# A sliding-window attention and a long convolution in one kernel: two transfers moved between queues, longer stage rings and a new order of steps

## The chip, the cores and the metric

The kernel runs on one core of a Trainium2 chip. The core has five engines that each take their instructions in order: TensorE (PE) for matrix products, whose weight loads the profile lists apart as PEld, VectorE (DVE), ScalarE (ACT), GpSimd (POOL) and SyncE (SP), which only issues transfers. The metric is the device time of one execution in microseconds (us). An engine stops at an instruction until what that instruction waits for is there, and everything behind it on that engine stops too.

## What is computed

Two independent parts, side by side in the output's columns.

```python
# A: 32 heads of 18, window of 8 positions, every second one
qkv = x @ wqkv                       # x: 2048 x 576
logits[s, w] = (q[s] . k[s - 2 * w]) * 18 ** -0.5     # masked where s - 2 * w < 0
a = (softmax(logits) weighted sum of v[s - 2 * w]) @ wo
# B: a shifted product, then a causal convolution over all 2048 positions
k_shift = sum over t < 4 of k[s - t] * shift_k[:, t]
kv = k_shift * v
y = irfft(rfft(kv, 4096) * rfft(ssm_k, 4096))[:2048] + kv * ssm_D
b = q * y
out = concatenate([a, b], axis=-1)   # 2048 x 1152, bf16
```

## The kernel before

The work is cut into some 400 short steps. Each is a function, and the text `ORDER` at the top lists them as the program is to emit them: `ks.3.0:a` calls `k_spec(3, 0)`, and the letters behind the colon choose the PSUM buffers (a or b, two of each) and the engine that copies the result out (s is ACT, v is DVE, and without either the step's own default, mostly ACT). The loop at lines 667 to 672 walks through this text. Nothing is sorted afterwards: on every engine, and on SyncE's queue, the instructions stand in the order of the text.

**Part A.** `xt` transposes x; `qk` and `qt` project q and k; `v` projects v, one step for two of the 18 elements of a head, into V, whose 16 columns in front of each block of positions are a halo, copied by `vh` (line 393) from the block before. `lm` multiplies q by shifted k on DVE (full ones of 128 x 4096 for h = 0 and 1, a half one for h = 2), `lb` sums the products into logits on PE. `sm` is the softmax, in steps 0 to 6 for each half `hv` of the columns: step 3 subtracts the maximum, step 4 is the exponential on ACT, 5 the sum on PE and its reciprocal on ACT, 6 the scaling on DVE. `pm` multiplies v by the weights (DVE, 128 x 4096, ring Pr of three), `ps` sums that on PE, nine of each for each half. `po` is the output projection for one quarter of the output, 72 pairs of products with one row group each, two copies out of PSUM and two stores from the ring sAr; `pz` is a `po` with the last two `ps` of half 1 put into it, four elements before its end.

**Part B.** The transforms are products with tables, in two stages. `cv` makes kv on DVE; `lkn`, `kw` and `kt` turn ssm_k around through DRAM. `sx` and `kp` are stage one of kv and of ssm_k: three steps each for eight groups, copied into a ring of two (vsr), and the third step writes the group to DRAM (Dx, Dk, line 439). `xl` and `kl` read these back in another layout (lines 546 and 547), into a ring of four slots (Wr) that `yl` shares. A read of Dk needs all eight groups of k to be written. `xs` and `ks` (line 536 on) are stage two, eight of each in two halves; `gp` multiplies the two spectra on DVE; `gi` is the first stage of the inverse, and its second half writes to Dy (line 581). `yl` reads Dy, four reads for each half of the channels, and each of these needs the four writes of its half; `ql` loads q into a ring of four; `ys` is the last stage, two steps for each of the eight, with the product with q on DVE (line 654) and, in the second, the store to the output from the ring ysr.

The order around the change: the first halo copy needs three `v` steps; `gi` needs `gp`, which needs `ks` and `xs`; a `po` needs all `ps` of its half. The last stage-one step of k is `kp.5.2`, and behind it in PE's order come `xs.5.0`, `xs.3.0`, `v.0`, `sm.1.5`, `xs.5.1`, `xs.3.1`, `v.8`, `sm.0.5`, `ps.1.0`, and then `ks.3.0`, the first step that reads k's stage one. At the end stand `ys.5.0` and `ys.5.1`.

Of the kernel before, what the change touches and what calls it, by code (L numbers as in the profile page):

```python
# [15 lines left out]


ORDER = """
tj lx.0.0 lx.0.1 lx.2.0 lwq.1.0 lx.1.0 lx.2.1 lwt lx.1.1 lwq.1.1 lwq.0.1 tv lk.0 lx.3.0 t2 sk.0:a t0 lk.2 sk.2:bv
lx.3.1 sk.1:b xt.0.1:bs xt.0.0:as xt.0.2:bs wm.11:a xt.2.2:as t3 xt.1.2:bs xt.1.0:as qk.1.0.0:b lk.1 xt.2.1:as  # L20
xt.1.1:as xt.2.0:bs t1 tw lwq.0.0 cv.0.0 cv.0.1 t4 qk.1.1.0:b wt qk.1.1.1:a t5 lv.0 lwv lkn.8 lkn.2 lkn.12 lkn.9 lk.3
lkn.13 lkn.4 qk.1.1.2:b xt.3.2:bs qk.0.1.0:a cv.0.3 lkn.6 xt.3.1:bs lkn.7 cv.0.4 lkn.5 lv.1 kw.6 cv.0.2 cv.0.5
xt.3.0:as cv.1.4 cv.0.6 cv.1.0 qk.0.0.2:b cv.1.1 kw.4 lkn.10 cv.0.7 kw.3 qk.0.1.2:b cv.1.3 lkn.14 qk.0.0.1:a sx.0.0:a
sx.0.1:b cv.3.3 cv.1.2 qk.1.1.3:b lkn.15 lkn.0 sx.0.2:a cv.1.5 sx.1.0:a lkn.11 qk.0.1.3:b cv.3.4 sx.1.1:b qt.3:a lkn.1
sx.1.2:b cv.2.1 kw.7 lkn.3 ld qk.0.1.1:a qt.0:b cv.1.6 cv.2.3 kw.0 kw.5 cv.2.4 cv.1.7 qk.0.0.3:b cv.2.0 cv.2.2
sx.2.0:a cv.2.5 kw.2 kw.1 qt.2:b cv.3.5 sx.2.1:a cv.2.6 sx.2.2:b kt.0 cv.3.1 qk.1.0.2:a sx.3.0:b sx.3.1:a kt.1
sx.3.2:b cv.3.0 qt.1:a qk.0.0.0:b qk.1.0.1:a qk.1.0.3:b kp.0.0:a lv.2 cv.3.2 lm.0.2 cv.3.6 kp.0.1:b lm.6.2 lv.3
kp.0.2:a lm.6.1 kp.1.0:b lm.6.0 cv.2.7 kp.1.1:b kp.1.2:a lm.0.0 v.4:a lb.6:a kt.3 kt.2 sx.4.0:b sx.4.1:a lm.0.1 lm.7.0
ia.3 sx.4.2:a sx.5.0:b sx.5.1:b v.2:a ia.5 lb.0:a ia.1 sx.5.2:b kp.2.0:b kt.4 cv.3.7 kp.2.1:a vz kp.2.2:a kt.7 lm.7.1
ia.0 lm.1.0 v.7:b lb.7:b lm.4.1 sx.6.0:a ib sx.6.1:a sx.6.2:b v.1:b sx.7.0:a lm.1.1 sx.7.1:b lm.2.2 sx.7.2:b lb.1:a  # L30
ia.2 lm.4.2 kp.7.0:a lm.4.0 kp.7.1:b xl.3 kp.7.2:b lm.2.1 v.5:a lb.4:b kt.6 kp.3.0:b lm.2.0 kp.3.1:a lm.3.0 kp.3.2:b
im.0 v.3:a kt.5 xl.5 lb.2:b kp.4.0:a kp.4.1:b kp.4.2:b lm.3.1 xl.6 im.1 v.6:a lb.3:a ia.7 kp.6.0:a kp.6.1:b lm.5.0
kp.6.2:a kp.5.0:b lm.5.1 lb.5:av kp.5.1:a sm.1.0 sm.1.1 kp.5.2:b sm.1.2 sm.1.3 xs.5.0:a sm.1.4 xs.3.0:bv ia.4 sm.0.0
v.0:a vh.1 sm.0.1 sm.1.5:a sm.0.2 xs.5.1:a sm.0.3 sm.0.4 xs.3.1:b v.8:a sm.1.6 pm.1.0 pm.1.6 kl.3 sm.0.5:a ps.1.0:b
ks.3.0:a pm.1.3 vh.0 ks.3.1:b gp.3.0 kl.5 gp.3.1 sm.0.6 ps.1.6:a kl.2 ks.5.0:b ks.5.1:a ps.1.3:b pm.0.0 lwo.0 xl.2
kl.0 ks.2.0:a vh.2 ks.2.1:b ia.6 xl.0 lwo.3 gi.3.0:a gi.3.1:b ps.0.0:a gp.5.0 xs.2.0:b gi.5.0:a gp.5.1 pm.1.1 gi.5.1:b
gp.2.0 pm.1.4 xs.2.1:b gp.2.1 ks.0.0:a pm.0.3 xs.6.0:b xl.1 gi.2.0:a ks.0.1:b kl.6 ql.1 xs.0.0:a xs.0.1:b kl.1 lwo.1
gp.0.0 gi.2.1:a ps.1.1:b gp.0.1 ps.0.3:a pm.0.8 xs.1.0:b pm.0.7 gi.0.0:a ks.6.0:b xs.6.1:a kl.7 ps.1.4:bv gi.0.1:a
ks.1.0:b pm.0.1 ks.6.1:a gp.6.0 xl.4 ps.0.7:b gp.1.0 ps.0.8:b ql.3 pm.0.4 xs.1.1:a ks.1.1:b gi.6.0:a ps.0.1:b kl.4
gi.1.0:a gp.6.1 gp.1.1 pm.1.5 pm.0.6 ks.7.0:b xl.7 ql.2 lwo.2 xs.4.0:a gi.1.1:b ps.0.4:a ql.0 ks.4.0:b gi.6.1:a pm.0.5  # L40
xs.7.0:b ps.1.5:av xs.7.1:b ks.7.1:a yl.2 xs.4.1:b ps.0.5:a ps.0.6:b gp.7.0 ks.4.1:a yl.3 yl.1 gi.7.0:b gp.4.0
gi.4.0:a pm.0.2 gp.4.1 yl.0 ps.0.2:b gp.7.1 gi.4.1:a gi.7.1:bv ys.2.0:as ys.2.1:b ys.3.0:as ql.4 ys.3.1:a pm.1.2 yl.4
ql.7 po.0.0.0:v pm.1.8 yl.7 pm.1.7 po.0.1.0 ps.1.2:a ys.0.0:bs ys.0.1:as po.0.0.1:v yl.6 pz.1.0.0 ys.4.0:as ql.6
ys.4.1:as ys.1.0:bs ys.1.1:a ql.5 yl.5 po.1.0.1:v po.1.1.0 ys.7.0:b ys.6.0:as ys.7.1:as ys.6.1:b po.1.1.1:v po.0.1.1
ys.5.0:a ys.5.1:bs
"""


# [1 line left out]
def kernel(  # L50
# [47 lines left out]
    def psb():  # L98
        return psum("b", 2, 512)

    def evac(dst, src, scale=None, on="s"):
        if (how["ev"] or on) == "s":
            nc.scalar.activation(dst, src, ACT.Copy, **({} if scale is None else {"scale": scale}))  # L103
# [442 lines left out]
    def w_load(Dd, key, i):  # L546
        nc.sync.dma_start(Wr.get((key, i)), by_rt(Dd, i // 4, i % 4))
# [20 lines left out]
    def g_inv(i, hv):  # L568
        dh, g = i // 4, i % 4
        Y = Yr[i] if hv else Yr.get(i)  # L570
        for u in range(2):
# [8 lines left out]
        if hv:  # L580
            nc.gpsimd.dma_start(by_rt(Dy, dh, g), Y)
# [121 lines left out]
```

## Time and profile before

| What | us |
|---|---|
| median of 3 runs (208.14 to 210.05) | 208.29 |
| the profiled execution | 211.04 |
| its span | 209.1 |
| PE starts at / its last product ends at | 5.86 / 204.1 |
| granted clock of PE over the span (share of full) | 0.999 |

The span is the profiled execution's time from its first to its last instruction. Busy time is the time in which an engine executes; an instruction that waits is not counted. A line of the waits names the engine and line that waited, what it waited for, the total, the number of times and the longest. In the timeline a line is a run of instructions of one form: start, length, engine, line, operation and tiles, then the idle time before it and what ended that. Line 103 is the helper that copies out of PSUM on ACT, line 105 the same on DVE, so these are told apart by tile sizes and times. The DMA issues give the median time from the issue to the landing of the data.

| Idle of PE by stretch | us |
|---|---|
| 0 to 6 | 5.9 |
| 6 to 52 | 0.3 |
| 52 to 70 | 2.2 |
| 70 to 120 | 4.2 |
| 120 to 160 | 4.0 |
| 160 to 180 | 0.6 |
| 180 to 192 | 0.9 |
| 192 to the end | 5.9 |

### The profile page before, as it was taken

What the parts mean: (1) busy time and instruction counts of PE and PEld (TensorE: products, weight loads), DVE (VectorE), ACT (ScalarE), POOL (GpSimd) and SP (SyncE); (2) the same over time, 40 slices, a digit from 0 to 9 for tenths busy, and PEclk for the clock granted to TensorE, in tenths of its full rate; (3) what the DMA queues carried; (4) which work ended last, traced back from release to release, by engine and by line L of the source; (5) the groups of instructions that cost most, each with busy time, mean ns of one, the idle gap of its engine ahead of it and who ended that gap; (6) DMA issues with size and microseconds to landing.
All of it is one profiled execution on the core that took longest, in us unless ns stands there. A gap on an engine that the chain in (4) does not pass through costs nothing.

```text
span 209.1 us, 6223 instructions
## 1 busy us (share of the span) xinstructions
PE 185.2 (89%) x2645; PEld 118.3 (57%) x2645; DVE 177.8 (85%) x157; ACT 160.7 (77%) x244; POOL 12.9 (6%) x39
## 2 busy tenths in 40 slices
...
GB/s 162 317 316 396 239 211 158 311 198 299 275 368 247 260 181 261 241 214 367 261 250 226 264 242 240 310 350 246 256 390 246 179 330 377 248 335 304 223 314 135
DMA packets 66797, 56.20 MB, mean 269 GB/s; under 512 B 16673, under 2 KB 60306, under 8 KB 66770
## 3 DMA queue, kind: packets, MB, share of 16 engines
...
## 4 chain that ended last, share of the span: by engine, by line
PE 46%; ACT 27%; DMA 16%; issue 6%; DVE 2%; SPq 0%; ACTq 0%; DVEq 0%
ACT area L103 24%; PE psB L377 8%; PE psA L377 5%; DMA Dx<-area 5%; PE psA L610 5%; DMA out_dram<-area 4%; DMA Dy<-area 4%; PE psA L384 3%; PE psA L576 3%; PE psB L599 3%; PE psB L432 2%; DMA Dk<-area 2%; PE psA L599 2%; PE psA L432 2%; DMA area<-in_B_shift_k_dram 2%
## 5 line engine op out<-in xcount | busy, mean ns | idle before, releaser
L103 ACT ACTIVATE area<-psA 128x576 bf16<-128x576 f32 (+7 forms) x117 | 83.5, 757 | 33.1 <-PE psB L610 15.0
L103 ACT ACTIVATE area<-psB 128x576 bf16<-128x576 f32 (+5 forms) x113 | 80.2, 757 | 7.9 <-PE psB L377 4.0
L588 DVE TENSOR_TENSOR area<-area,area 128x4096 bf16<-128x4096 bf16 x18 | 40.6, 2284 | 0.9 <-DMA area<-area 0.8
L487 DVE TENSOR_TENSOR area<-area 128x4096 bf16<-128x4096 bf16 x16 | 35.8, 2286 | 1.0 <-PE psA L504 0.7
L377 PEld LDWEIGHTS <-area 128*128 128x128 bf16 x160 | 15.5, 98 | 17.5
L377 PE MATMUL psB<-area,area 128*128 128x512 bf16 x100 | 23.1, 379 | 0.0
L563 DVE TENSOR_TENSOR area<-area 128x2304 bf16<-128x2304 bf16 x16 | 21.1, 1351 | 1.3 <-ACT area L103 1.0
L461 DVE TENSOR_TENSOR area<-area,area 128x2304 bf16<-128x2304 bf16 x16 | 21.0, 1348 | 0.0
L541 PEld LDWEIGHTS <-W 128*64 128x64 bf16 x256 | 14.0, 108 | 12.3 <-issue 11.1
L610 PE MATMUL psA<-area,area 32*128 32x288 bf16 x288 | 18.7, 281 | 1.6 <-ACT area L103 1.1
L610 PE MATMUL psB<-area,area 32*128 32x288 bf16 x288 | 18.7, 281 | 0.0
L384 PEld LDWEIGHTS <-area 128*32 128x32 bf16 x360 | 15.2, 142 | 5.6 <-issue 2.8
L599 PEld LDWEIGHTS <-ident 64*64 64x64 bf16 x576 | 15.3, 106 | 5.1 <-issue 3.5
L610 PEld LDWEIGHTS <-area 32*128 32x128 bf16 x576 | 15.5, 93 | 4.6 <-issue 2.2
L384 PE MATMUL psA<-area,area 128*32 128x512 bf16 x280 | 16.7, 384 | 0.4 <-ACT area L103 0.2
L432 PEld LDWEIGHTS <-T 128*128 128x128 bf16 x96 | 8.6, 97 | 14.6 <-issue 9.3
L541 PE MATMUL psB<-area,W 128*64 128x288 bf16 x152 | 14.7, 290 | 1.8 <-ACT area L103 1.1
L455 DVE TENSOR_TENSOR area<-area,area 128x2304 bf16<-128x2304 bf16 x12 | 15.8, 1350 | 0.1
L576 PEld LDWEIGHTS <-IAt 64*128 64x128 bf16 x256 | 12.4, 94 | 5.8 <-issue 1.5
L432 PE MATMUL psB<-area,T 128*128 128x384 bf16 x52 | 12.6, 326 | 3.5 <-ACT area L103 3.5
L377 PE MATMUL psA<-area,area 128*128 128x512 bf16 x60 | 13.9, 379 | 0.0
L576 PE MATMUL psA<-area,IAt 64*128 64x288 bf16 x176 | 13.0, 283 | 0.4
...
## 6 DMA issues: line engine op xcount, KB each, us to landing
Dx<-area SPq DMA_DIRECT2D x16, 288.0 KB, 4.2
Dk<-area SPq DMA_DIRECT2D x16, 288.0 KB, 4.4
area<-Dx SPq DMA_DIRECT2D x8, 576.0 KB, 5.9
area<-Dk SPq DMA_DIRECT2D x8, 576.0 KB, 6.8
Dy<-area POOLq DMA_DIRECT2D x8, 576.0 KB, 6.2
area<-Dy SPq DMA_DIRECT2D x8, 576.0 KB, 6.2
area<-in_A_wo_dram SPq DMA_DIRECT2D x4, 648.0 KB, 10.2
area<-in_A_x_dram SPq DMA_DIRECT2D x8, 288.0 KB, 5.4
```

Source lines behind the costliest of these rows:

```text
L103: nc.scalar.activation(dst, src, ACT.Copy, **({} if scale is None else {"scale": scale}))
L377: nc.tensor.matmul(ps[:, u, :], w[:, kb, cols[u]:cols[u] + 128], xT[:, j, kb], start=(kb == 0), stop=(kb == 4))
L384: nc.tensor.matmul(ps[32 * a:32 * a + 32, u, :], wv[:, kb, 2 * n + u:D:DH], xT[:, a, kb], start=(kb == 0), stop=(kb == 4), tile_position=( ...
L432: nc.tensor.matmul(ps[:, ri, 0:384], T1[:, ri, :], sf[:, 384 * ch:384 * ch + 384], start=True, stop=not extra)
L461: nc.vector.tensor_tensor(dst, kfull[:, 4 * c + 3 - j:4 * c + 7 - j, :], skb[:, j, :].unsqueeze(1).to_broadcast([128, 4, D]), ALU.mult)
L487: nc.vector.tensor_tensor(prr.get((n, h)), q2[h], k2[h][:, :, o0:o0 + S], ALU.mult)
L541: nc.tensor.matmul(ps[64 * hp:64 * hp + 64, im, 0:HD], W2[:, im, 8 * g + 2 * prl + hp].rearrange("p l f -> p (l f)"), Wt[:, 2 * prl + hp, ...
L563: nc.vector.tensor_tensor(Pv, Xv.unsqueeze(2).to_broadcast([128, 2, 2, 2 * HD]), Kv.unsqueeze(1).to_broadcast([128, 2, 2, 2 * HD]), ALU.mult)
L576: nc.tensor.matmul(ps[:, hp, 0:HD], IAt[r, tab, 4 * g + 2 * hv + u, :], Pp[(i, hv)][r, n, u, :], start=(n == 0), stop=(n == 3), tile_posit ...
L588: nc.vector.tensor_tensor(Pr.get((hv, p)), vv, Lt[:, :, 256 * hv:256 * hv + 256].unsqueeze(2).to_broadcast([128, W, 2, 256]), ALU.mult)
L599: nc.tensor.matmul(ps[64 * b:64 * b + 64, r, 0:256], ident[g, g], P[g, n, :, 128 * b:128 * b + 128], start=(n == 0), stop=(n == W - 1), ti ...
L610: nc.tensor.matmul(pss[e][:, b, 0:HD], Os[hv][g, d // 2, r, 128 * (d % 2):128 * (d % 2) + 128], wo4[g, d, d0:d1], start=(d == 0), stop=(d ...
```

## The change

Two transfers change their queue: the three halo copies of V and the eight writes of the inverse's first stage are issued from SyncE, where before GpSimd issued them. The ring of stages for the second output's last products has four slots where it had two, and that of the projection's copies has nine where it had six; the new slots lie in an area that the kernel did not use any more at that time. The list of steps holds the same steps in another order, some of them with another PSUM buffer or another engine for the copy.

```diff
 ORDER = """
...
-kp.6.2:a kp.5.0:b lm.5.1 lb.5:av kp.5.1:a sm.1.0 sm.1.1 kp.5.2:b sm.1.2 sm.1.3 xs.5.0:a sm.1.4 xs.3.0:bv ia.4 sm.0.0
-v.0:a vh.1 sm.0.1 sm.1.5:a sm.0.2 xs.5.1:a sm.0.3 sm.0.4 xs.3.1:b v.8:a sm.1.6 pm.1.0 pm.1.6 kl.3 sm.0.5:a ps.1.0:b
-ks.3.0:a pm.1.3 vh.0 ks.3.1:b gp.3.0 kl.5 gp.3.1 sm.0.6 ps.1.6:a kl.2 ks.5.0:b ks.5.1:a ps.1.3:b pm.0.0 lwo.0 xl.2
...
-gi.4.0:a pm.0.2 gp.4.1 yl.0 ps.0.2:b gp.7.1 gi.4.1:a gi.7.1:bv ys.2.0:as ys.2.1:b ys.3.0:as ql.4 ys.3.1:a pm.1.2 yl.4
-ql.7 po.0.0.0:v pm.1.8 yl.7 pm.1.7 po.0.1.0 ps.1.2:a ys.0.0:bs ys.0.1:as po.0.0.1:v yl.6 pz.1.0.0 ys.4.0:as ql.6
-ys.4.1:as ys.1.0:bs ys.1.1:a ql.5 yl.5 po.1.0.1:v po.1.1.0 ys.7.0:b ys.6.0:as ys.7.1:as ys.6.1:b po.1.1.1:v po.0.1.1
-ys.5.0:a ys.5.1:bs
+lx.1.0 lx.1.1 tj t0 lx.3.1 t2 lx.3.0 xt.1.2:as tv lx.0.1 sk.0:b xt.1.0:as sk.1:a xt.3.0:bs lx.2.1 lx.2.0 t3 lx.0.0
+wm.11:b lwt xt.1.1:a sk.2:b xt.2.2:bs xt.2.0:as xt.0.1:bs lwq.1.1 xt.0.0:bs tw xt.2.1:a qk.1.1.1:a lk.0 xt.0.2:bs
...
+kp.6.1:bv kp.6.2:a lb.4:a lm.5.1 im.0 kp.7.0:b kp.7.1:a xl.3 kp.7.2:b v.5:a kp.3.0:a lm.2.1 kp.3.1:bv lb.2:b kp.3.2:a
+vh.2 kl.3 im.1 kl.0 xs.0.0:b lm.5.0 lm.3.0 vh.1 v.1:a lb.5:a xs.3.0:b ia.4 lm.3.1 xs.3.1:av lb.3:b xs.0.1:b ks.3.0:b
+ks.0.0:a sm.1.0 sm.0.0 sm.1.1 ib sm.0.1 sm.1.2 sm.1.3 sm.1.4 gp.3.0 ql.6 v.2:b kl.1 ql.3 sm.0.2 gp.0.0 xl.1 sm.1.5:a
+vh.0 sm.0.3 sm.1.6 ks.3.1:b gi.0.0:a gp.3.1 sm.0.4 pm.1.2 xs.1.0:b gi.3.0:a sm.0.5:b pm.1.0 sm.0.6 ks.0.1:a lwo.1
+gp.0.1 kl.5 ql.2 pm.0.8 xs.1.1:b ps.1.2:a ia.6 lwo.2 ks.1.0:b xl.5 gi.0.1:a gp.1.0 ks.5.0:b kl.2 pm.0.1 gi.3.1:a
+ks.5.1:b xl.6 ps.1.0:a pm.0.2 ks.1.1:b gp.1.1 ps.0.8:a xs.5.0:b gi.1.0:a xs.5.1:b pm.0.0 xl.2 ps.0.1:a kl.4 gi.1.1:b
...
+ps.0.3:b ps.0.6:a gp.2.0 gp.2.1 gi.2.0:b ql.1 kl.7 xs.4.0:av ks.4.0:b gp.6.1 pm.0.7 gi.2.1:a ks.4.1:b gi.6.1:a
+xs.4.1:b xs.7.0:av ps.0.7:b gp.4.0 xs.7.1:a ks.7.0:b yl.1 gp.4.1 pm.1.1 yl.0 yl.2 ks.7.1:a gi.4.0:b gp.7.0 gi.4.1:a
+ps.1.1:b gp.7.1 po.0.0.1 yl.3 ys.1.0:b pm.1.3 gi.7.0:a gi.7.1:b ys.2.0:as ys.1.1:bs ql.0 pm.1.5 po.0.1.1 pm.1.4
+po.0.1.0 yl.7 ys.0.0:as ys.3.0:bs ys.2.1:as ps.1.4:b ps.1.3:b pm.1.8 ql.7 yl.4 ps.1.5:b ys.3.1:a ys.0.1:bs pm.1.7 yl.6
+ql.5 yl.5 ql.4 po.0.0.0 pz.1.0.0:s ys.7.0:a po.1.1.1 ys.6.0:b ys.4.0:as ys.7.1:a ys.6.1:bs ys.4.1:bs ys.5.0:a ys.5.1:b
+po.1.0.1 po.1.1.0
 """
...
-    ysr = Ring(mk.take(4, HD), mk.take(4, HD))
+    r9.reset()
+    ysr = Ring(mk.take(4, HD), mk.take(4, HD), r9.take(4, HD), r9.take(4, HD))
     smt = [mk.take(2304) for _ in range(2)]
-    sAr = Ring(*[r.take(2, HD) for r in (r1, r5, r6, r1, r5, r6)])
+    sAr = Ring(*[r.take(2, HD) for r in (r1, r5, r6, r1, r5, r6, r9, r9, r9)])
...
     def v_halo(g):
         d = slice(6 * g, 6 * g + 6)
-        nc.gpsimd.dma_start(V[32:128, d, 0:PADL], V[0:96, d, 512:VT])
+        nc.sync.dma_start(V[32:128, d, 0:PADL], V[0:96, d, 512:VT])
...
         if hv:
-            nc.gpsimd.dma_start(by_rt(Dy, dh, g), Y)
+            nc.sync.dma_start(by_rt(Dy, dh, g), Y)
             Yr.drop(i)
```

Copies that the new order gives to DVE: `xt.1.1`, `xt.2.1`, `kp.0.1`, `sx.7.0`, `kp.6.1`, `kp.3.1`, `xs.3.1`, `xs.4.0` and `xs.7.0`, and those of seven `ys` steps. In the old order these were `sk.2`, `lb.5`, `xs.3.0`, `ps.1.4`, `ps.1.5`, `gi.7.1`, the four `po` with a v, the last `ps` inside `pz`, and those of six `ys` steps.

More of the change, by code (lines that the diff above doesn't have):

```diff
@@ L18 @@
 ORDER = """
[L19 to L32, printed above, removed]
-kp.6.2:a kp.5.0:b lm.5.1 lb.5:av kp.5.1:a sm.1.0 sm.1.1 kp.5.2:b sm.1.2 sm.1.3 xs.5.0:a sm.1.4 xs.3.0:bv ia.4 sm.0.0
@@ L34 @@
-v.0:a vh.1 sm.0.1 sm.1.5:a sm.0.2 xs.5.1:a sm.0.3 sm.0.4 xs.3.1:b v.8:a sm.1.6 pm.1.0 pm.1.6 kl.3 sm.0.5:a ps.1.0:b
-ks.3.0:a pm.1.3 vh.0 ks.3.1:b gp.3.0 kl.5 gp.3.1 sm.0.6 ps.1.6:a kl.2 ks.5.0:b ks.5.1:a ps.1.3:b pm.0.0 lwo.0 xl.2
-kl.0 ks.2.0:a vh.2 ks.2.1:b ia.6 xl.0 lwo.3 gi.3.0:a gi.3.1:b ps.0.0:a gp.5.0 xs.2.0:b gi.5.0:a gp.5.1 pm.1.1 gi.5.1:b
-gp.2.0 pm.1.4 xs.2.1:b gp.2.1 ks.0.0:a pm.0.3 xs.6.0:b xl.1 gi.2.0:a ks.0.1:b kl.6 ql.1 xs.0.0:a xs.0.1:b kl.1 lwo.1
-gp.0.0 gi.2.1:a ps.1.1:b gp.0.1 ps.0.3:a pm.0.8 xs.1.0:b pm.0.7 gi.0.0:a ks.6.0:b xs.6.1:a kl.7 ps.1.4:bv gi.0.1:a
@@ L39 @@
-ks.1.0:b pm.0.1 ks.6.1:a gp.6.0 xl.4 ps.0.7:b gp.1.0 ps.0.8:b ql.3 pm.0.4 xs.1.1:a ks.1.1:b gi.6.0:a ps.0.1:b kl.4
-gi.1.0:a gp.6.1 gp.1.1 pm.1.5 pm.0.6 ks.7.0:b xl.7 ql.2 lwo.2 xs.4.0:a gi.1.1:b ps.0.4:a ql.0 ks.4.0:b gi.6.1:a pm.0.5
-xs.7.0:b ps.1.5:av xs.7.1:b ks.7.1:a yl.2 xs.4.1:b ps.0.5:a ps.0.6:b gp.7.0 ks.4.1:a yl.3 yl.1 gi.7.0:b gp.4.0
-gi.4.0:a pm.0.2 gp.4.1 yl.0 ps.0.2:b gp.7.1 gi.4.1:a gi.7.1:bv ys.2.0:as ys.2.1:b ys.3.0:as ql.4 ys.3.1:a pm.1.2 yl.4
-ql.7 po.0.0.0:v pm.1.8 yl.7 pm.1.7 po.0.1.0 ps.1.2:a ys.0.0:bs ys.0.1:as po.0.0.1:v yl.6 pz.1.0.0 ys.4.0:as ql.6
@@ L44 @@
-ys.4.1:as ys.1.0:bs ys.1.1:a ql.5 yl.5 po.1.0.1:v po.1.1.0 ys.7.0:b ys.6.0:as ys.7.1:as ys.6.1:b po.1.1.1:v po.0.1.1
-ys.5.0:a ys.5.1:bs
+lx.1.0 lx.1.1 tj t0 lx.3.1 t2 lx.3.0 xt.1.2:as tv lx.0.1 sk.0:b xt.1.0:as sk.1:a xt.3.0:bs lx.2.1 lx.2.0 t3 lx.0.0
+wm.11:b lwt xt.1.1:a sk.2:b xt.2.2:bs xt.2.0:as xt.0.1:bs lwq.1.1 xt.0.0:bs tw xt.2.1:a qk.1.1.1:a lk.0 xt.0.2:bs
+lwq.0.0 xt.3.2:bs qk.1.1.2:a cv.0.0 cv.0.3 lwq.0.1 t4 lwq.1.0 qk.0.0.2:b wt qk.0.0.0:a lk.1 cv.0.1 lwv xt.3.1:bs lk.2
+t1 cv.0.4 cv.1.4 cv.0.5 lv.0 ia.2 cv.0.2 qt.2:a lv.1 qk.0.1.0:a cv.0.6 cv.1.3 lkn.6 cv.0.7 cv.1.1 lkn.4 lkn.7 lkn.14
@@ new lines @@
+lk.3 lkn.12 cv.1.0 lkn.15 cv.2.3 cv.1.2 kw.3 qk.0.0.3:b cv.1.5 lkn.0 cv.2.1 qk.1.0.1:a lv.2 lkn.1 lkn.8 kw.7 sx.0.0:b
+cv.1.6 lkn.9 sx.0.1:a qt.3:b cv.1.7 cv.3.4 sx.0.2:a qk.1.0.0:b cv.2.4 kw.0 qt.1:a lkn.10 sx.1.0:a lkn.11 sx.1.1:b
+v.0:b lkn.5 sx.1.2:b cv.2.0 cv.3.3 cv.2.2 cv.2.5 qk.0.1.3:a sx.2.0:a cv.3.1 lkn.2 sx.2.1:b kw.5 ld kw.2 qk.1.0.2:b
+sx.3.0:a lkn.13 kw.4 lkn.3 sx.2.2:b cv.2.6 qk.1.1.0:a qk.0.1.2:a cv.3.5 kw.6 cv.2.7 sx.3.1:b kw.1 ia.1 sx.3.2:a cv.3.0
+qk.0.0.1:b kt.1 cv.3.2 sx.4.0:a vz kt.0 qk.1.0.3:b qt.0:b cv.3.6 lm.6.0 lv.3 sx.4.1:a sx.4.2:a lm.0.2 lm.0.0 t5
@@ new lines @@
+qk.0.1.1:b ia.5 kp.1.0:a kp.1.1:a kp.1.2:b cv.3.7 qk.1.1.3:b kp.0.0:a kt.2 kp.0.1:av kp.0.2:b lm.0.1 v.3:b lm.6.2 ia.3
+sx.5.0:a lb.0:b kt.4 sx.5.1:b lm.6.1 ia.7 sx.5.2:a lm.7.0 sx.6.0:a sx.6.1:b sx.6.2:b lb.6:a lm.7.1 ia.0 v.7:a
+sx.7.0:bv kt.5 lm.1.0 sx.7.1:a sx.7.2:b lb.7:a kp.2.0:b kp.2.1:a kp.2.2:b xl.0 kt.6 lm.4.2 lm.1.1 v.4:a kp.4.0:b
+kp.4.1:a kp.4.2:b v.6:a lm.4.0 lb.1:a kp.5.0:b kp.5.1:b lm.2.2 kt.7 kp.5.2:a lm.4.1 v.8:a lm.2.0 kp.6.0:b kt.3
+kp.6.1:bv kp.6.2:a lb.4:a lm.5.1 im.0 kp.7.0:b kp.7.1:a xl.3 kp.7.2:b v.5:a kp.3.0:a lm.2.1 kp.3.1:bv lb.2:b kp.3.2:a
```

2 lines of the change are left out of this document (added).

## The prediction

> **What bounds the kernel now.** I read the page's busy times first, then the engines' busy time by stretches of the span, the waits (the SyncE queue's own too), the DMA issues, and last the timeline at two places. Engine totals:
>
> ```profile
> PE 185.2 (89%) x2645; PEld 118.3 (57%) x2645; DVE 177.8 (85%) x157; ACT 160.7 (77%) x244; POOL 12.9 (6%) x39
> ```
>
> No engine is idle enough to be free. Where the time is lost shows in the stretches (length, then busy time of PE, PEld, DVE, ACT, POOL):
>
> ```profile
> 6.00:52.00 46.00, 45.66 (x266) 23.96 (x265) 40.59 (x48) 37.85 (x48) 0.92 (x5) 1.00 1.08 271
> ...
> 70.00:120.00 50.00, 45.82 (x660) 29.12 (x660) 45.80 (x32) 45.09 (x64) 2.37 (x3) 1.00 0.99 252
> 120.00:160.00 40.00, 36.02 (x634) 25.34 (x635) 37.97 (x24) 38.70 (x72) 2.74 (x5) 1.00 1.02 283
> 160.00:180.00 20.00, 19.44 (x427) 15.17 (x426) 18.53 (x18) 14.05 (x26) 1.60 (x3) 1.00 0.93 296
> ```
>
> Until 52 us TensorE (PE) is the bound. From 70 to 160 three engines are above 90% and PE loses 8.2 us to the others; from 120 to 160 ScalarE (ACT) is at 97%, VectorE (DVE) at 95%. After 170 PE leads again. So a new order gains only where it removes waits between engines that are all nearly full. The waits the edits aim at:
>
> ```profile
> POOL Dy L581 <- ACT area L103: 50.8, 7, 10.7
> ...
> DVE area L654 <- DMA out_dram<-area: 4.2, 2, 2.1
> ...
> ACT area L103 <- DMA out_dram<-area: 1.0, 1, 1.0
> ```
>
> The first is GpSimd waiting in front of the inverse's writes, for results that ACT has not yet copied; nothing else is queued there. The others are the two stages of the second output, held by their stores. What a write followed by a read through DRAM costs (KB each, us to landing):
>
> ```profile
> Dk<-area SPq DMA_DIRECT2D x16, 288.0 KB, 4.4
> ...
> area<-Dk SPq DMA_DIRECT2D x8, 576.0 KB, 6.8
> Dy<-area POOLq DMA_DIRECT2D x8, 576.0 KB, 6.2
> area<-Dy SPq DMA_DIRECT2D x8, 576.0 KB, 6.2
> ```
>
> And one such passage in the timelines of PE and SyncE, from the last stage-one product of k to the first spectrum of k:
>
> ```profile
> 103.07 0.49 PE L432 MATMUL psB<-area,T 128*128 128x384 bf16 x2
> ...
> 102.72 4.07 SPq L439 DMA_DIRECT2D Dk<-area  x4
> ...
> 108.59 3.70 SPq L547 DMA_DIRECT2D area<-Dk  x3
> ...
> 115.61 0.71 PE L541 MATMUL psA<-area,W 128*64 128x288 bf16 x8
> ```
>
> The product ends at 103.5, its write is out at 106.8, the first read starts at 108.6, and ks.3.0 runs at 115.6: 12.1 us.
>
> **Three stages.** I cut the span at the start of ks.3.1 (116.1), the end of gi.7.1 (171.8) and the last matmul (204.1); the last store ends it at 209.1. So 116.1 + 55.7 + 32.3 + 5.0. For each stage I add each engine's steps in both orders. Durations are from start to start on a full engine: on PE, 2.2 for a v, 1.2 for an lb, 0.70 for an xs or ks, 1.03 for a gi, 1.02 for a ps, 2.23 for a po, 0.52 for a ys, 0.98 for the softmax sum; on ACT, 0.69 for a 768-wide copy, 1.06 for the two of an xs, ks, gi or po, 0.49 for a ps; on DVE, 2.2 for a pm or a full lm, 1.27 for a gp, 0.67 for a 576-wide copy.
>
> **First stage.** PE now starts on quarter 1's transposes. Their two loads are issued first, at 0.8 and 1.3; with the 5.4 us that x loads take they are there at 6.3 to 6.7, where before PE began at 5.86: +0.5. Two transposes' copies and four stage-one copies go to DVE. DVE has no 768-wide row: 0.69 for 512 and 0.75 for 576 put it at 0.9; the least is 0.75, the most 1.5 for two 576s. ACT is relieved of 4 x 0.69 = 2.8, of which I count 1.0 on the path (none to 2.8), since DVE is as full. Ahead of k's last product the new order has the same number of v steps (seven) but two lb fewer: -2.4. So that product ends at 103.5 + 0.5 - 1.0 - 2.4 = 100.6.
>
> Here lies the main cost. Before, PE had xs.5.0, xs.3.0, v.0, sm.1.5, xs.5.1, xs.3.1, v.8, sm.0.5 and ps.1.0 to do in the 12.1 us: 10.2 of work. Now it has xs.0.0, v.1, lb.5, xs.3.0, xs.3.1, lb.3 and xs.0.1: 7.4, and ks.3.0 stands in front of v.2 and sm.1.5. PE idles 4.7 in place of 1.9. vh.2's halo copy, now on SyncE, stands between the write and the read, but SyncE waits 1.8 there for the write anyway, and its issue (0.36 to 1.6 among SyncE's rows, 0.75 on GpSimd) mostly fits. ks.3.0 is at 112.7; with ks.0.0, v.2 and sm.1.5 (4.6 with ks.3.0), ks.3.1 comes at 117.3. [...]
>
> **Second stage.** PE before: 27 xs or ks, 16 gi, 14 ps = 49.7. After: 26, 16, 13, and sm.0.5, po.0.0.1 and ys.1.0: 51.7. ACT: 50.4 before (27 and 15 doubles, 12 ps), 52.5 after (24 and 16 doubles, 13 ps, a softmax exponential, po's copies). DVE up to what gi.7.1 needs: 49.1 before, 51.0 after (xs.4.0 and xs.7.0 add 2.7). Before, the stage took 5.3 more than its fullest engine's sum. ACT is still the fullest; 52.5 + 4.5 = 57.0, a little less than 5.3 because ACT and PE are closer to even. From 54.5 (2 over the sum) to 59.5.
>
> The eight inverse writes now cost SyncE 8 x 0.5 (the Dx rows) = 4.0 of issue. SyncE is idle in waits for far longer, so that is hidden. What counts is that SyncE stands at each until ACT has copied: behind gi.0.1 waits kl.2, behind gi.3.1 xl.6, behind gi.5.1 xl.7, behind gi.6.1 yl.1. Counting PE work between where a load can be issued and its use, kl.2, xl.6 and xl.7 keep over 8 us, more than the 6.8 they take: nothing. xl.2, which waits for a slot and not for a write, keeps 5.5, about a microsecond short: in the range. Landing should be as from GpSimd: same-sized reads on SyncE take 5.9 to 6.8, against 6.2.
>
> **Third stage.** PE: 29.2 before; 28.5 after (15 ys, 7 po, 5 ps). The trace took 3.1 more. More stages remove the idle PE had at 197 to 199, 0.9 us; nine projection stages are worth nothing, since no projection copy waits for a store. But ql.0 now needs the slot that ys.1.1 frees, and its product comes two pm later: 0.45 + 6.9 - 4.4 = 3.0 of DVE idle, and pm.1.8 and pm.1.7 are behind it. DVE then needs 14.0 and a lag of 1.2 from ys.1.1 to the end of pm.1.7; PE has 14.1 before the sum that needs it: 1.1 late. 28.5 + 3.1 - 0.9 + 1.1 = 31.8. The end: a po's two copies (1.3) and a store (3.6) take what ys.5.1 took: 5.0.
>
> **Sum.** 117.3 + 57.0 + 31.8 + 5.0 = 211.1, against a span of 209.1: +2.0. (The profiled execution lasted 211.04 with 1.9 around its span; the median of the runs is 208.29.) 208.3 + 2.0 = 210.3.
>
> **Rivals.** *Faster: the loads land early.* The Dk read's shortest row is 4.9 and ACT may lag 1.3 instead of 2.4; then the passage is 9.1, and PE, which lb.3 holds for some 1.4 until DVE's lm.3.1, is hardly idle: -3.0. With a second stage at its lower bound, -2.5: 204.8. For it: ACT is lighter; against: three engines above 90% seldom drop to 2 us of loss. [...]
>
> *Slower: SyncE's order holds y.* yl.1 needs Dy of gi.2.1: ACT's lag 1.5, issue 0.5, write 6.2, issue 0.4, read 6.2 = 14.8; with the longest rows (7.8, 8.1) 18.3. PE has 11.6 of work from gi.2.1 to ys.1.0, 12.8 with the stage's usual idle. Beyond that everything stops, since gi.7.0, gi.7.1 and pm.1.3 are behind ys.1.0. 2.0 to 5.5, of which I have counted some 0.5 in the second stage: +3.0, 213.3. Before, gi.1.1 had over 14 us to ys.2.0. [...]
>
> *Nothing: the waits removed and added cancel,* as they would with a k read of 5.5: 208.5.
>
> **Chances.** Forecast 0.40 (208.5 to 212), half of it beyond 1%; faster 0.28; slower 0.24; nothing 0.08. A measurement of this kernel tells about 1% from no change, so: faster 0.28, same 0.28, slower 0.44. The range, with the unknown bounds on both sides, is 204.5 to 214.5.
>
> **What would show it.** Right: a gap of 3 us or more on PE ahead of the first ks, a DVE wait of 2 to 3 us for q in the tail, no DVE or ACT wait on a store. Wrong: ks.3.0 running straight after xs.0.1, or ACT under 90% between ks.3.1 and gi.7.1 with PE full.

## The result, and the profile after

| What | before | after |
|---|---|---|
| median of four executions, us | 209.04 | 215.94 |
| lowest to highest | 208.14 to 210.05 | 214.28 to 217.30 |
| profiled execution / its span | 211.04 / 209.1 | 216.25 / 214.5 |
| start of ks.3.1 | 116.1 | 115.3 |
| from there to the end of gi.7.1 | 55.7 | 62.3 |
| from there to the last matmul | 32.3 | 31.0 |
| from there to the end | 5.0 | 6.0 |

The time after is 1.0325 times the time before, 95% interval 1.023 to 1.042. Each ratio below is against executions of the kernel before on the same chip at the same time, and leaves out executions over 1.5% above their kernel's fastest, which the kernel before shows too (9 of 26 in one series); where that took several of a new kernel's, they are listed. The whole loss is in the second stage. The engines' busy time over the span has hardly changed:

```profile
PE 186.5 (87%) x2645; PEld 115.7 (54%) x2645; DVE 176.5 (82%) x152; ACT 162.3 (76%) x248; POOL 6.1 (3%) x28
```

The stretches of after (length, then PE, PEld, DVE, ACT, POOL busy, granted clock, the DMA engines' busy share, GB/s; that share is the packets' time over that of 16 engines and passes 1 in the first row), first those that were shown of before, then slices of 2 us:

```profile
6.00:52.00 46.00, 44.38 (x291) 23.44 (x290) 42.95 (x45) 35.88 (x46) 0.60 (x4) 1.00 1.10 285
70.00:120.00 50.00, 43.98 (x594) 24.73 (x587) 47.04 (x34) 42.49 (x60) 0.00 (x0) 1.00 0.93 251
120.00:160.00 40.00, 34.06 (x634) 24.45 (x635) 39.00 (x24) 35.77 (x67) 0.00 (x0) 0.98 0.99 279
160.00:180.00 20.00, 19.12 (x340) 13.44 (x340) 12.86 (x13) 16.29 (x30) 0.00 (x0) 0.95 0.64 203
...
156.00:158.00 2.00, 0.00 (x0) 0.00 (x0) 2.00 (x4) 0.00 (x0) 0.00 (x0) 1.00 0.94 346
158.00:160.00 2.00, 1.27 (x10) 0.78 (x11) 2.00 (x2) 0.54 (x1) 0.00 (x0) 0.68 0.11 35
160.00:162.00 2.00, 2.00 (x18) 1.05 (x16) 0.28 (x1) 1.31 (x3) 0.00 (x0) 0.50 0.00 0
```

In 160 to 180 PE did 340 matmuls where it did 427 before. At 156 to 158 it did none, and from 158.7 to 162.1 it ran at half clock. PE's timeline there (start, length, operation, count, idle before and what ended it):

```profile
154.91 0.68 PE L542 MATMUL psA<-area,W 128*64 128x288 bf16 x8
158.73 1.17 PE L542 MATMUL psB<-area,W 128*64 128x288 bf16 x8 [3.14 <-issue]
159.84 2.10 PE L577 MATMUL psA<-area,IAt 64*128 64x288 bf16 x16
```

The idle time stands ahead of ks.4.0, and its releaser is "issue": no data, no slot and no copy that the profile knows of. The k that it reads was asked for at 135.4. The gi behind it took 2.10 us, where others take 1.15.

Of the waits that the edits aimed at, DVE's and ACT's for stores are gone from the list. The inverse writes' wait now stands on SyncE, shorter than the 50.8 us on GpSimd:

```profile
SPq L582 <- ACT area L103: 28.1, 8, 11.4
```

The transfers' rows (KB each, us to landing): the writes of k and Dy land earlier than before, the reads of x later.

```profile
Dk<-area SPq DMA_DIRECT2D x16, 288.0 KB, 3.9
area<-Dx SPq DMA_DIRECT2D x8, 576.0 KB, 7.6
area<-Dk SPq DMA_DIRECT2D x8, 576.0 KB, 6.7
Dy<-area SPq DMA_DIRECT2D x8, 576.0 KB, 4.9
area<-Dy SPq DMA_DIRECT2D x8, 576.0 KB, 5.7
area<-in_A_wo_dram SPq DMA_DIRECT2D x4, 648.0 KB, 8.6
```

What "issue" hides can be read from the DMA queues. One of them is named "instruction":

```profile
q1 hardware_dynamic: 68448, 55.81, 94.0%
q8 instruction: 20, 0.33, 0.7%
```

It carries 20 packets of 16,384 B in the span. Between two of their starts PE does 256 matmuls and weight loads on average, and the 20 of them cover nearly all of its 5,290, so they are read here as PE's own instructions, piece by piece. Call each matmul or weight load a row, and count the requests from 0: at quiet times request j starts where PE runs row 202 + 256 j (202 fitted to the trace of before; 33 of the 40 requests of before and after started no more than 2.5 us behind that point). Request 11 of after started at 156.25, 6.1 us behind that point, and PE had stopped at 155.6 with its 1,629th matmul, 240 rows past the point: by this reading it had nothing left to run. Every trace here has the same stop. In none of 17 did PE start the next row sooner than 1.2 us after the end of that request's packet (323 cases), and 25 times it stood for 0.3 to 3.7 us exactly there and went on 1.2 to 1.7 us after that end (four more times it went on over 3.3 us after, with a copy of ACT's as the releaser). SyncE's queue, what it had issued in the 10 us ahead:

```profile
146.35 0.32 SPq L582 DMA_DIRECT2D Dy<-area  x1
146.72 1.68 SPq L273 DMA_DIRECT2D area<-in_A_wo_dram  x1
149.16 0.32 SPq L548 DMA_DIRECT2D area<-Dx  x1
149.58 0.38 SPq L642 DMA_DIRECT2D area<-in_B_q_dram  x1
150.07 1.26 SPq L548 DMA_DIRECT2D area<-Dk  x1
```

A write, the 648 KB of `lwo.0` (one of four loads of the projection's weights, which have their places in the list of steps) and three more loads, about 2.6 MB, lie ahead of the request at 150.

### The profile page after: what moved, and what is told of

The parts are those of the page before. It is cut to its first block, busy times and chain, and to the rows that moved or that the text cites. A ratio compares the mean times of both kernels' runs of the same rounds, so it can differ in the third digit from the quotient of the medians.

```text
span 214.5 us, 6194 instructions
## 1 busy us (share of the span) xinstructions
PE 186.5 (87%) x2645; PEld 115.7 (54%) x2645; DVE 176.5 (82%) x152; ACT 162.3 (76%) x248; POOL 6.1 (3%) x28
## 4 chain that ended last, share of the span: by engine, by line
DMA 30%; PE 22%; ACT 22%; SPq 8%; DVE 8%; issue 7%; ACTq 1%; DVEq 0%
ACT area L103 19%; DMA area<-Kt 5%; PE psA L611 5%; DMA Dx<-area 4%; DMA area<-in_B_v_dram 4%; DMA area<-in_B_k_dram 4%; SPq L263 4%; DMA Dk<-area 3%; PE psA L577 3%; DMA area<-Dk 3%; DMA area<-in_A_x_dram 2%; DVE area L589 2%; PE psB L600 2%; DVE area L462 2%; ACT area L527 2%
## 5 line engine op out<-in xcount | busy, mean ns | idle before, releaser
L103 ACT ACTIVATE area<-psA 128x576 bf16<-128x576 f32 (+6 forms) x110 | 78.5, 743 | 29.3 <-PE psB L611 9.9
L103 ACT ACTIVATE area<-psB 128x576 bf16<-128x576 f32 (+8 forms) x124 | 85.5, 731 | 14.5 <-PE psB L542 3.7
L462 DVE TENSOR_TENSOR area<-area,area 128x2304 bf16<-128x2304 bf16 x16 | 21.2, 1353 | 0.6 <-DMA area<-in_B_k_dram 0.4
L542 PE MATMUL psB<-area,W 128*64 128x288 bf16 x168 | 16.5, 300 | 5.5 <-issue 3.1
L378 PE MATMUL psA<-area,area 128*128 128x512 bf16 x80 | 18.6, 379 | 1.5 <-ACT area L103 1.5
L378 PE MATMUL psB<-area,area 128*128 128x512 bf16 x80 | 18.6, 379 | 0.0
L385 PEld LDWEIGHTS <-area 128*32 128x32 bf16 x360 | 13.5, 141 | 6.7 <-issue 2.4
L456 DVE TENSOR_TENSOR area<-area,area 128x2304 bf16<-128x2304 bf16 x11 | 14.6, 1353 | 0.1
L385 PE MATMUL psA<-area,area 128*32 128x512 bf16 x240 | 14.3, 383 | 0.0
L577 PE MATMUL psA<-area,IAt 64*128 64x288 bf16 x176 | 13.8, 298 | 0.0
L433 PE MATMUL psB<-area,T 128*128 128x384 bf16 x48 | 11.4, 327 | 2.0 <-DVE area L105 0.8
```

The source lines that it names most:

```text
L378: nc.tensor.matmul(ps[:, u, :], w[:, kb, cols[u]:cols[u] + 128], xT[:, j, kb], start=(kb == 0), stop=(kb == 4))
L385: nc.tensor.matmul(ps[32 * a:32 * a + 32, u, :], wv[:, kb, 2 * n + u:D:DH], xT[:, a, kb], start=(kb == 0), stop=(kb == 4), tile_position=( ...
L433: nc.tensor.matmul(ps[:, ri, 0:384], T1[:, ri, :], sf[:, 384 * ch:384 * ch + 384], start=True, stop=not extra)
L462: nc.vector.tensor_tensor(dst, kfull[:, 4 * c + 3 - j:4 * c + 7 - j, :], skb[:, j, :].unsqueeze(1).to_broadcast([128, 4, D]), ALU.mult)
L542: nc.tensor.matmul(ps[64 * hp:64 * hp + 64, im, 0:HD], W2[:, im, 8 * g + 2 * prl + hp].rearrange("p l f -> p (l f)"), Wt[:, 2 * prl + hp, ...
```

## The experiments

### Is it the instructions?

**wo_moved.** The load in front is moved away.

```diff
-... sm.0.6 ks.0.1:a lwo.1
+... sm.0.6 ks.0.1:a lwo.1 lwo.0
-... xs.6.1:b lwo.0 xl.7 ...
+... xs.6.1:b xl.7 ...
```

> One load is moved: lwo.0, the projection's weights of group 0 (648 KB), stands right behind lwo.1 and not ahead of xl.7. Theory (late instructions): PE's instructions come by DMA in pieces of 16 KB, 256 instructions each; the piece that ks.4.0 needs was asked for 6.1 us late, because the load lwo.0 lay in front of it, and PE ran dry. Then the gap of 3.4 us in ks.4.0 and the half clock after it go: no PE idle over 2 us between ks.3.1 and gi.7.1, granted clock 1.0 there, second stage 57 to 58 in place of 62.1, time 209.5 to 211.5. The request at about 118 may be late instead, but it has 6 us to spare. Rival (a wait of ks.4.0 for data, a slot or a copy): gap where it was, 215 to 217.

Measured: 211.48, 211.99, 215.81 and 217.12, against 208.91; the ratio of the two lower ones is 1.0157 (1.007 to 1.024). The profiled execution is the 217.12, so no trace shows one that gained: request 11 is 2.4 us late, PE has no gap at ks.4.0, the clock is full, and still the second stage takes 61.4. In it PE waits 2.0 us for Dk, 0.8 for Dx and ACT 1.1 for a write of Dy. The dry PE at ks.4.0 went with the load, and in this execution other waits took its place.

**rows_shifted.** The profile of after has a weight load for each of its matmuls (2,645 of both), so five matmuls fewer are ten rows.

```diff
-wm.11:b lwt xt.1.1:a
+wm.6:b lwt xt.1.1:a
```

> Five of the eleven warm-up matmuls of the first microseconds are left out (their result is read by nobody), so that every later PE instruction stands 10 rows earlier in the program. Theory (late instructions): the pieces of 256 are cut 10 rows later in the order of steps, so the gap moves: it opens inside ks.4.0 after some 5 of its matmuls instead of before the first, and stays 3 to 4 us long; time 214 to 217. Rival (a wait of ks.4.0's first matmul): the gap stays ahead of that matmul. Both expect the half clock behind the gap.

Measured: 216.41, 1.0365 (1.028 to 1.045). PE's timeline:

```profile
156.83 0.68 PE L542 MATMUL psA<-area,W 128*64 128x288 bf16 x8
157.35 0.68 PE L542 MATMUL psB<-area,W 128*64 128x288 bf16 x5
159.96 0.40 PE L542 MATMUL psB<-area,W 128*64 128x288 bf16 x3 [1.94 <-issue]
160.30 1.73 PE L577 MATMUL psA<-area,IAt 64*128 64x288 bf16 x16
```

The eight matmuls of ks.4.0 are cut in two, five ahead of the gap and three behind it, as the theory asks of a shift by five. A wait for data, a slot or a copy can't do that: it would stand ahead of the first or, for the second of the step's two PSUM buffers, of the fifth. The gap was again followed by half clock (160.7 to 164.1).

**halo_pool.** Only the halo copies go back to GpSimd.

```diff
-        nc.sync.dma_start(V[32:128, d, 0:PADL], V[0:96, d, 512:VT])
+        nc.gpsimd.dma_start(V[32:128, d, 0:PADL], V[0:96, d, 512:VT])
```

> The kernel after with the halo copies back on GpSimd; the inverse writes stay on SyncE. In the run with both on GpSimd the halo copy landed late and DVE stood 3.0 us for it ahead of pm.1.2. Theory (late instructions behind the burst at 146, which the inverse write on SyncE makes; halo late as well): the gap in ks.4.0 as in after, and DVE's wait for the halo beside it: 215 to 218. Rival (the halo copy on SyncE is what costs the time, as in the run with the order kept): 210 to 212.

Measured: 216.95, 1.0369 (1.028 to 1.046), as the theory said. The gap stands at the same matmul (profiled at 218.85):

```profile
158.48 0.68 PE L542 MATMUL psA<-area,W 128*64 128x288 bf16 x8
162.87 1.17 PE L542 MATMUL psB<-area,W 128*64 128x288 bf16 x8 [3.71 <-issue]
```

The request was 6.2 us late. DVE waited 2.3 us for a halo copy. The nine profiles in the new order, by how late request 11 was (the profile puts the idle time of pool_queue and wo_late down to ACT, but both end 1.4 us after the packet):

```
kernel        request 11 late   idle of PE at that row
halo_pool          6.2                3.7
after              6.1                3.1
rows_shifted       5.3                1.9
pool_queue         4.2                1.2
wo_late            3.6                0.7
wo_moved           2.4                none
dy_pool_wo         2.4                none
wo_pieces          2.4                none
after_no_wo        1.9                none
```

### What the queues and the rings do

**pool_queue.** Both transfers go back to GpSimd, in the new order.

```diff
-            nc.sync.dma_start(by_rt(Dy, dh, g), Y)
+            nc.gpsimd.dma_start(by_rt(Dy, dh, g), Y)
```

and the halo copies as in halo_pool.

> The order and rings of after, but the halo copies and the inverse writes go out from GpSimd as before. Theory (late instructions): SyncE no longer stands 4 to 11 us at the writes, so loads are issued when their slot is free, one by one and not in a burst at 146 to 151; lwo.0 goes out several us earlier and clear of the request at 150: gap gone, 209.5 to 212. Rival (the order itself makes ks.4.0 wait): gap of 3 us stays, 215 to 217. Rival (SyncE's order as such costs time beyond the gap): under 209.

Measured: 211.41, 214.88, 215.27 and 215.75, too far apart for a ratio. The theory's gap-free 209.5 to 212 is missed: request 11 was still 4.2 us late. The profiled execution (215.75) lost more elsewhere: DVE waited 3.0 us for a halo copy, its products came late, and PE stood 2.9 us at a gi for them.

**order_kept.** The old list of steps with the new queues and rings (diff: ORDER of before).

> The queues and rings of after with the order of steps of before. Theory (late instructions, set by where the projection's weights and the inverse writes fall in the new order): no gap over 2.5 us on PE between ks.3.1 and gi.7.1; time 207.5 to 210, since the rings take away the stores' waits in the third stage (0.9) and little else changes. Rival (the moved writes hold SyncE and cost the time whatever the order): 212 to 216.

Measured: 212.67, 1.0224 (1.013 to 1.032): the rival's number, and by one clear wait. SyncE's queue and PE, in that kernel:

```profile
SPq L394 <- DVE area L589: 3.9, 1, 3.9
```

```profile
111.43 0.61 SPq L394 DMA_DIRECT2D area<-area  x1
112.15 1.04 SPq L548 DMA_DIRECT2D area<-Dk  x2
```

```profile
118.76 1.17 PE L542 MATMUL psB<-area,W 128*64 128x288 bf16 x8 [3.32 <-DMA area<-Dk]
```

SyncE stood 3.9 us at a halo copy until DVE was done; the two k reads behind it went out late, and PE waited 3.3 us for one of them. 6.8 us of half clock followed.

**rings_only.** Old order, old queues, the larger rings alone.

> The order and queues of before with only the two larger rings (four stages for ys, nine for po). Theory (the rings take away the waits on stores in the third stage and nothing else): 207.5 to 209, no wait of DVE or ACT on a store. Rival (a ring changes where other waits fall, as the whole change did): over 211.

Measured: 210.10, 1.0031 (0.999 to 1.007): no difference that the measurement can tell. The waits on stores are gone. In the profiled execution, the slowest of the ten, ACT waited 2.3 us for a write of Dy near 133; why the 0.9 does not show in the other nine is open.

**kept_halo_pool.** As rings_only, with the inverse writes on SyncE.

> The order of before, the larger rings, the inverse writes on SyncE, but the halo copies on GpSimd as before. It parts the two queue moves in the run with the order kept, where SyncE stood 3.9 us at vh.0 for DVE and the k reads behind it came late: PE waited 3.3 us for Dk at 115.4 and two windows of half clock followed. Theory (the halo copy held SyncE): no such wait, no half clock inside the span, 208 to 210. Rival (the inverse writes hold SyncE): 211 to 214 as with both.

Measured: 210.62, 1.0078 (1.003 to 1.013). So in the old order the halo copies on SyncE cost some 3 us (order_kept against this one, 3.8 and 0.7 above their references), and the eight inverse writes about 1 or nothing: the intervals of this kernel and of rings_only overlap. The half clock did not go, though: it stands once, from 105.7, behind 2.1 us in which PE waited for ACT.

### What else can be late

**dy_pool_wo.** wo_moved, with the inverse writes on GpSimd.

> The order and rings of after with lwo.0 right behind lwo.1, the inverse writes on GpSimd, the halo copies on SyncE. Theory (late instructions from the burst behind the inverse write, and, with both transfers on GpSimd, a late halo copy that held DVE 3.0 us): neither is left, so no PE idle over 2 us between ks.3.1 and gi.7.1, all executions near 209.5 to 211.5. Rival (the new order itself is some 3 us longer in the second stage): 212 to 215 with no single gap.

Measured: 216.67, 1.0329 (1.025 to 1.041), all executions between 216.2 and 218.2. Both are missed, by the time and by the single gap: ACT stood 2.8 us because a stage of gi was still being written to Dy, PE stood behind it, and half clock followed (139.2 to 142.7). The last write ahead of that had gone out at 131.5; a weight load and three other loads had in the 10 us before. That they made it late is likely, not shown.

**wo_pieces.** The four weight loads in three parts each, the twelve spread over the list from ks.0.1 to kl.7.

```diff
-    def load_wo(g):
-        nc.sync.dma_start(wo4[32 * g:32 * g + 32], A_wo.rearrange("(h d) n -> h d n", d=DH), max_dma_last_dim=2304)
+    def load_wo(g, k):
+        d = slice(6 * k, 6 * k + 6)
+        nc.sync.dma_start(wo4[32 * g:32 * g + 32, d], A_wo.rearrange("(h d) n -> h d n", d=DH)[:, d, :], max_dma_last_dim=2304)
```

> The kernel after with each of the four loads of the projection's weights (648 KB) cut into three of 216 KB, which are spread over the order from the place of lwo.1 to that of kl.7. The same bytes, no long load. Theory (a long load holds up the requests for instructions): no request after 115 us is late by over 4 us, no dry PE in ks.4.0; 209.5 to 212, and no execution over 214. Rival (the traffic as such makes them late, or something other than lwo.0): 213 to 217.

Measured: 215.91, 1.0311 (1.023 to 1.039): the rival. No request after 115 us was over 3.5 us late, and PE did not run dry at ks.4.0. In place of that it waited for operands:

```profile
143.53 0.68 PE L543 MATMUL psB<-area,W 128*64 128x288 bf16 x8 [2.84 <-DMA area<-Dx]
...
151.97 0.80 PE L543 MATMUL psB<-area,W 128*64 128x288 bf16 x8 [3.00 <-DMA area<-Dk]
```

So the instructions were the victim in after, not the cause. Something makes one transfer or another late by 3 us whichever way the loads are laid. The stretches of before show a candidate that the prediction had in front of it and passed over (the last two columns: the DMA engines' busy share, GB/s):

```profile
115.00:158.00 43.00, 38.57 (x698) 27.46 (x692) 40.97 (x26) 41.67 (x78) 3.64 (x6) 1.00 1.02 286
158.00:172.00 14.00, 13.58 (x258) 9.68 (x256) 12.87 (x9) 13.53 (x25) 1.10 (x3) 1.00 0.88 249
```

And of after:

```profile
115.00:158.00 43.00, 36.62 (x676) 25.98 (x674) 41.88 (x28) 40.00 (x73) 0.00 (x0) 1.00 1.02 287
158.00:172.00 14.00, 12.72 (x184) 8.38 (x183) 9.43 (x8) 11.18 (x21) 0.00 (x0) 0.88 0.49 164
```

The DMA engines are full until 158 in both (1.02). The old order still keeps them busy after that (0.88), the new one does not (0.49, and 0.57 in wo_moved, where PE does not stand at ks.4.0): it asks for its loads sooner, in a stretch in which the engines are already full.

**before_wo_pair and before_wo_three.** The old order with weight loads pushed together at 138 us.

```diff
-... xs.0.1:b kl.1 lwo.1
+... xs.0.1:b kl.1 lwo.1 lwo.2
```

and for the second `kl.1 lwo.3 lwo.1 lwo.2`, each taken from its old place.

> The kernel before with one load moved the other way: lwo.2 goes out right behind lwo.1 (at about 138 in place of 152), so that 1.3 MB is under way when PE asks for the piece of instructions after 144. Theory (late instructions): that request, 1.1 us late before, is 4 to 8 us late, PE runs dry near 150 for 1 to 3 us with no data, slot or copy as releaser, and a window of half clock may follow; 210 to 215. Rival (loads do not hold up instructions): 207.5 to 210, no such gap; if kl.7 lands late instead, PE waits for Dk there.

> The kernel before with three of the four weight loads in a row (lwo.3, lwo.1, lwo.2, 1.9 MB from about 138 us). With two in a row the request for instructions after 144 was 3.4 us late and had 1.6 us to spare. Theory (late instructions): late by over 5 us now, PE dry at its 1,500th matmul, near 150 us, for 1 to 4 us, with no data, slot or copy as releaser; 210.5 to 215. Rival (loads do not hold up instructions): no gap at that matmul, or one that Dk or Dx releases; 208 to 211.

Measured: 210.92, 1.0018 (0.997 to 1.007), and 212.65, 1.0205 (1.013 to 1.028). Two executions of the pair's ten are left out (212.52 and 212.74). The request after 144 came 3.4 and 3.7 us late. PE ran dry where the theory said, near its 1,500th matmul, with "issue" as the releaser, but for 0.4 us in the first and 0.9 in the second, less than the 1 us that was the least expected. The line of the second:

```profile
148.19 0.41 PE L599 MATMUL psB<-area,ident 64*64 64x256 bf16 x8 [0.90 <-issue]
```

So the mechanism shows in the old order too, and its price there was set too high. A larger wait of the second: a write of Dy came late and held ACT for 2.0 us.

**after_no_wo, before_no_wo, before_more.** Loads taken out of the stretch, and put in.

```diff
-        nc.sync.dma_start(wo4[32 * g:32 * g + 32], A_wo.rearrange("(h d) n -> h d n", d=DH), max_dma_last_dim=2304)
+        if g == 1:
+            nc.gpsimd.memset(wo4.rearrange("p d n -> p (d n)").bitcast(FP32), 0.0)
```

in the first two, and in before_more, to the order of before:

```diff
-... pm.0.7 gi.0.0:a ks.6.0:b ...
+... pm.0.7 gi.0.0:a lwo.0 ks.6.0:b ...
-gi.1.0:a gp.6.1 gp.1.1 ...
+gi.1.0:a lwo.3 gp.6.1 gp.1.1 ...
```

> The kernel after without the four loads of the projection's weights (2.6 MB between 115 and 155 us): GpSimd sets them to zero instead, so the first output is zeros. All instructions of PE, ACT and DVE stay. Theory (the DMA engines are full between 115 and 158, and the new order asks for more there than they bring): requests for instructions are at most 3 us late, no PE idle over 2 us between ks.3.1 and gi.7.1, no half clock, 208 to 211. Rival (the new order as such): a gap of the same size, 214 to 217.

> The control: the kernel before without the four weight loads, zeros from GpSimd in their place. Theory (the DMA engines are full here too, but the order of before is fitted to it): a gain smaller than in the new order, 206.5 to 208.5. If the new order is as good as the old one but for the traffic, the two come out within 2 us of each other; if it is worse in itself, it stays 4 us or more above.

> The kernel before with two of the weight loads made twice (lwo.0 again behind lwo.1, lwo.3 again ahead of xl.7): 1.3 MB more between 138 and 158 us, with nothing computed in another way. Theory (the DMA engines' capacity): instructions, Dk, Dx or a write of Dy come late, a gap of 2 to 4 us on PE, perhaps half clock: 211 to 216. Rival (traffic is hidden): 208 to 210.

Measured: after_no_wo 212.03, 1.0161 (1.008 to 1.025); before_no_wo (its projection is zeros too) 207.71, 0.9952 (0.991 to 0.9995, without 210.76 and 211.76); before_more 216.65, 1.0418 (1.031 to 1.053). The stretch of after_no_wo:

```profile
115.00:158.00 43.00, 39.12 (x709) 27.62 (x710) 41.88 (x27) 42.20 (x77) 3.08 (x1) 1.00 0.70 222
```

With the DMA engines at 0.70, no request in the second stage is over 2.0 us late, PE has no gap over 2 us there, and the stage takes 58.0 in place of 62.3. The time is above the 211 that I expected at most. One reason is in the tail: request 17 was 4.1 us late there, PE ran dry for 1.8 us, and half clock followed. The other is the order, which costs something without the loads too: the two kernels without them are 4.3 us apart, more than the 4 that were to mark the order as worse in itself. (Without the loads SyncE is also spared their issue, 1.7 us for lwo.0; no run parts that from the traffic.) The converse holds in the old order. With 1.3 MB more between 138 and 158 us, all else being equal, it loses as much as the change did, at a Dx read:

```profile
162.05 1.17 PE L541 MATMUL psB<-area,W 128*64 128x288 bf16 x8 [3.51 <-DMA area<-Dx]
```

**wo_late.** The same bytes as after, one load later.

```diff
-... xs.6.1:b lwo.0 xl.7 ...
+... xs.6.1:b xl.7 ...
-... pm.0.7 gi.2.1:a ks.4.1:b ...
+... pm.0.7 gi.2.1:a lwo.0 ks.4.1:b ...
```

> The kernel after with lwo.0 put off: it goes out behind the inverse write of gi.2.1 (about 156 us) in place of ahead of xl.7 (147); po.0.0.1, which reads it first, comes at 171. Theory (the DMA engines are asked for too much before 158 and are half idle until 172): requests for instructions up to ks.4.0 at most 4 us late, no dry PE there, no other operand late by over 2 us; 210 to 212.5, as without the loads at all. Rival (any wait of one load moves the loss to another, as with lwo.0 ahead and with the loads in pieces): 214 to 217.

Measured: 212.39, 212.63, 212.75, 212.93, and two executions at 215.66 and 216.57; the ratio of the four is 1.0173 (1.012 to 1.023). The stretches:

```profile
115.00:158.00 43.00, 37.88 (x696) 26.63 (x692) 41.19 (x27) 41.04 (x75) 0.00 (x0) 1.00 0.91 264
158.00:172.00 14.00, 12.61 (x238) 9.19 (x236) 10.95 (x9) 11.30 (x21) 0.00 (x0) 1.00 0.92 274
```

The load is spread evenly now (0.91 and 0.92). The request after 150 is 3.6 us late and the one before it 4.9, more than the 4 expected, so PE still runs dry, but for 0.6 and 0.7 us only, and no half clock follows. The second, in ks.4.0:

```profile
156.26 0.68 PE L542 MATMUL psB<-area,W 128*64 128x288 bf16 x8 [0.69 <-ACT area L103]
```

Most of what leaving the loads out had gained is there with all of them made. No kernel tried here that does all the work beats the one before.

## Why the prediction was wrong

Predicted 210.3, measured 215.94.

| Part of the span | predicted | measured |
|---|---|---|
| to the start of ks.3.1 | 117.3 | 115.3 |
| second stage | 57.0 | 62.3 |
| third stage | 31.8 | 31.0 |
| the end | 5.0 | 6.0 |
| sum | 211.1 | 214.5 |

The spans miss by 3.4 us. The rest of the 5.6 is the reference: the 2.0 was added to a median of 208.29, but the sum was made against the profiled execution of before, which was 2.75 us longer, while that of after was 0.3 above its median.

**First stage: the mechanism was there, the sizes were not.** k's last product ended at 100.4 (predicted 100.6), which is luck: PE began at 4.0 and not at 6.3, and the terms of the sum behind its start brought some 2 us less than thought. The passage through DRAM took some 9 us in place of 12.1: the write landed in 2.5 us, the read for ks.3.0 was there within 4.9, and the one that ended last, for ks.0.0, took 5.87. So ks.3.0 ran right behind xs.0.1, at 109.4, PE was idle for 1.8 us in all between 100.4 and 111, and the gap of 3 us that was named as the sign of being right is missing. This is what the rival "the loads land early" said of this step (9.1 us). ks.3.0 was 3.3 us ahead of its forecast; 1.3 of these went on the way to ks.3.1 (5.9 us in place of 4.6), and the 2.0 gained are left.

**Second stage: the step that failed.** It read "52.5 + 4.5 = 57.0", with the loads' spare time counted against a fixed landing time ("over 8 us, more than the 6.8 they take: nothing"). The 4.5 was the idle of the old order carried over, and no one landing time held: the reads of Dx and Dk, 576 KB each, took 4.6 to 10.0 us in after (4.9 to 7.9 in before). The share of 1.02 stood in the prediction's own rows. There was no term for PE's instructions as a transfer among the others. The runs put in its place: 58.0 without the weight loads and 4.3 more with them, which the dry PE (3.1) and the half clock behind it (ks.4.0 and the gi took 1.4 longer) make up. before_more shows that the old order has no more room either.

That 57.0 comes near 58.0 is luck in part. Without the loads the old order's second stage takes 54.5, so the new one is 3.4 longer by itself, where the prediction had 1.3. Its own sums have 2.0 of that as more work for PE. What it had no term for is a wait ahead of sm.0.5, the softmax sum that the new order brings into this stage: 1.2 to 1.7 us in all nine traces of the new order, none in the old. PE waits there for a PSUM copy on ACT that stands behind sm.0.4's exponential (1.9 us). No run took this wait out, so what it costs is not shown.

On the clock: in after the half clock lasted 3.41 us, behind a gap of 3.1 us, and gaps of 2.1 to 2.8 us had it behind them too in kept_halo_pool, rings_only and dy_pool_wo. On the instructions: the pieces are of 16,384 B for 256 rows, and the late one cost PE 3.1 us.

**The moved writes.** That the issue of the eight writes is hidden holds to within about 1 us (kept_halo_pool against rings_only). Their landing, 4.9 us against 6.2, is not the queue's doing: from GpSimd in the new order it was 4.6 (pool_queue) and 4.2 (dy_pool_wo). The rival "SyncE's order holds y" fell: ahead of ys.1.0 PE waited 0.3 us. SyncE's order did hold something, but a halo copy, and only with the old list of steps (order_kept). "Mostly fits", said of vh.2's copy in the new order, held: the reads behind it went out at 104.5.

**Third stage.** DVE was idle for 2.15 us ahead of the product at 186.5 (predicted 3.0), and PE waited 0.9 us for DVE behind it (predicted 1.1); the waits on stores went (one of about 2 us stands in halo_pool and in pool_queue, with the same rings). The profile names a copy of ACT's as what ended that idle time, but in seven of the nine traces of the new order it puts the wait ahead of this product (1.4 to 2.5 us) down to the load of q, as predicted. The last store ended 6.0 us behind the last matmul, one more than thought.

**What stays open.** Of the 6.9 us between the medians, some 3 come back by moving one load later (3.1 by the medians, 3.2 by the ratios) and 3.4 to 3.9 by leaving the four out. The larger part is not the traffic of these loads: the two kernels without them differ by 4.3, where 2.0 had been predicted, with 1.0 in the first stage of their profiles, 3.4 in the second and 2.2 in the third, where one of the two ran dry for 1.8. Beyond that and the wait ahead of sm.0.5, what the order costs was not taken apart.
